# Matmuls of a constant ahead of PE's first work and in its early pauses, and the Gelu table first on ACT, in a linear-attention and feed-forward kernel

## Chip, core and metric

The kernel runs on one NeuronCore of a Trainium2 chip. The metric is device time in microseconds of one execution. Engines are named as in the profile: PE (TensorE matmul), PEld (its weight loads), DVE (VectorE), ACT (ScalarE), POOL (GpSimd), SP (SyncE, which here only issues transfers).

## The reference

A recurrent attention with a decaying state, for 4 batches, 8 heads, 768 steps and 48 dimensions per head, and a feed-forward layer with a sigmoid Gelu over the 3072 tokens of 384 features that it yields:

```python
for t in range(S):
    cur = einsum('bhd,bhe->bhde', u * k[t], v[t])
    y[t] = einsum('bhd,bhde->bhe', r[t], state + cur)
    state = w[t][..., None] * state + einsum('bhd,bhe->bhde', k[t], v[t])
x = y.transpose(0, 2, 1, 3).reshape(B * S, H * D)      # 3072 x 384
h = x @ w_in                                           # 384 x 2048
out = (h * sigmoid(1.702 * h)) @ w_out                 # 2048 x 384
```

## The kernel before

**Attention in chunks.** The 3072 steps are cut into 24 chunks of 128 steps, 6 for each batch, which follow one another through the state. Two heads share a tile, so a chunk has 4 pairs. `chunk(t)` is a Python generator of 11 pieces, the tokens `a<t>` of the order below: (1) a scan over the decays (L236) and a reciprocal; (2) a second scan (L242) and the product r*k (L249); (3) the scaled k and r (`kq`, L257 and L258), all on DVE; (4) eight matmuls of two columns (`ps_d`, L264), which read the masks `hm`; (5) the copy `s` of their result (L267) and the scaling of the state on DVE; (6) four transposes (`ps_t`, L280) and their copy `kt` on ACT (L282); (7) eight small products on ACT (`am`, L289); (8) the 64 small matmuls `ps_u` (L302, L308), then `mid` and the new state on DVE (L313, L316; for the first chunk of a batch `mid` on ACT); (9) a masked copy into `am` on DVE (L319); (10) the matmuls `ps_y` (L326 and half of L337) and a one-element copy on DVE that reads them (L346); (11) the other half of L337, and the split of the result into a high part (ACT, L202) and a low part (DVE, L203), which go to the tile `x`.

**Feed-forward.** Weights come in as pieces (`fetch`, tokens `f`), and are converted and split into high and low parts in four steps each (`convert`, tokens `w`: ACT L188 and L189, DVE L191 and L194, ACT L196, DVE L198). `first_product` (tokens `g`, 9 matmuls, L375 to L377) writes a PSUM tile `ph` out of two buffers; `gelu` (tokens `h`) reads it twice on ACT (L386, L387) and subtracts on DVE (L388); `second_product` (tokens `y`, 9 matmuls, L401 to L403) adds into `po`. The first tasks are 256 tokens wide, later ones 512. Tokens `m` are checks of magnitudes on ACT (L208), `l` are loads of a chunk, `M` is the load of the masks into `hm`, `x` moves rows of `x` to their places.

**Order.** Each engine runs its instructions in the order of the program. For the first 42 tasks that order is written by hand, in the string `RAMP` of tokens; after that a loop spreads the pieces over the tasks. A load's issue waits on the queue of its engine (SP, ACT or POOL), and later issues of that queue wait behind it.

**PSUM.** Three buffers serve all of the attention's tiles in turn (`ps_a`), two serve `ph`, three hold `po`.

**Before the order begins** POOL clears `hm`, the decays' helpers and others, DVE clears parts of two load buffers (L109, L110), and ACT runs one Gelu of a column of the mask `after` (L133), whose result nobody reads: it makes the table of functions be loaded early.

Of the kernel before, what the change touches and what calls it, by code (L numbers as in the profile page):

```python
# [8 lines left out]
F32 = mybir.dt.float32  # L9
F32R = mybir.dt.float32r  # L10
BF16 = mybir.dt.bfloat16
I32 = mybir.dt.int32
U32 = mybir.dt.uint32
AF = mybir.ActivationFunctionType
# [7 lines left out]
P = 128  # L22
# [3 lines left out]
R2 = HB + D  # L26
# [35 lines left out]

FIRST = 42
RAMP = """
l0 a0 l0 M a0 a0 l0 l1 m0 a0 f0 a0 a0 a1 a1 a0 a0 a0 m0 a1 a0 a1 a0 l1 f1 a1 a1 w0 l2 a1 m1 a1 w0 a1 a2 a1 a2
a2 w1 w0 a1 a2 a2 m1 a2 w1 m2 a2 l3 l2 a3 f2 a3 m2 w1 x1 w0 a2 a3 a3 w2 a2 f3 g0 w1 m3 l3 f4 a3 h0 g1 h1 a3 a2
y0 w3 y1 w2 w3 l4 a3 f5 a2 a3 a3 w2 m3 a3 w2 w3 a3 x3 g2 h2 w3 g3 h3 g4 y2 w4 a4 y3 f6 h4 w4 g5 w5 g6 h5 y4 w5
w4 g7 h6 w4 h7 a4 w5 y5 w5 g8 h8 w6 g9 y6 g10 y7 h9 y8 g11 f7 w6 w7 w7 h10 y9 g12 h11 w6 w6 g13 w7 l4 w7 h12
y10 h13 y11 g14 a4 f8 f9 w8 y13 g15 h14 y12 w9 l5 g16 w8 a4 h15 w9 w8 m4 w8 y14 y15 h16 g17 w9 a4 a4 g18 a5
h17 a5 f10 y16 h18 g19 g20 a5 a4 y17 w9 h19 w10 y18 w10 m4 f11 a4 l5 a5 a4 h20 l6 w11 w10 y19 l7 w11 g21 h21  # L70
m5 y20 g22 a5 w10 m5 a6 w11 a5 l6 a4 w11 a4 a5 g23 a6 a5 a5 y21 h22 a6 a6 m6 a5 a6 a7 l8 a5 a7 a6 y22 a6 a7 a6
m6 g24 a7 a6 l7 a7 h23 a7 a6 a6 a7 a7 a7 g25 l9 a7 h24 l8 a7 m7 a8 h25 y23 u a8 a8 x7 m7 y24 y25 l9 g26 m8 a8
h26 g27 h27 g28 a8 a8 y26 a8 y27 a9 a9 h28 g29 l10 y28 a8 g30 a9 m8 h29 a8 m9 g31 h30 a9 a9 l10 a9 a8 a10 a9
a8 y29 g32 y30 h31 y31 a10 a9 h32 l11 a9 g33 g34 l11 m9 a10 m10 h33 y32 g35 m10 a10 a10 a9 h34 a9 a10 l12 g36
a11 a11 y33 h35 a10 g37 a11 h36 y34 m11 h37 a10 a10 g38 a11 a11 g39 m11 a12 a10 l12 a12 a10 a12 a11 a12 a11
a12 y35 h38 y36 a11 l13 a11 a12 h39 g40 a11 m12 l13 a11 x11 y37 l14 m12 a12 y38 g41 y39 h40 a12 a13 h41 l14
"""
WIDE = 512
assert sum(CHUNKS) == NT
# [3 lines left out]
def rwkv_ffn_kernel(ctx: ExitStack, tc, wkr, vp, vrk, ub, w_in, w_out, masks, vt, uc, out):  # L83
    nc = tc.nc
    V, A, G, T = nc.vector, nc.scalar, nc.gpsimd, nc.tensor
# [4 lines left out]
    ps_h = ctx.enter_context(tc.tile_pool(name="ps_h", bufs=2, space=PSUM))  # L90
# [3 lines left out]
    at = fast.enter_context(tc.tile_pool(name="at", bufs=1))  # L94


    hm = cp.tile([R2, 2 + H], F32, name="hm")
# [6 lines left out]
    n = NP * CW + 1  # L104
# [10 lines left out]
    after = cp.tile([P, HB], F32, name="after")  # L115
# [14 lines left out]

    A.activation(at.tile([P, 1], F32, tag="s", name="junk", bufs=2), after[:, 0:1], AF.Gelu_apprx_sigmoid)  # L133

    wih, wil, woh, wol = (cp.tile([P, NF, DM], F32R, name=x) for x in ("wih", "wil", "woh", "wol"))
    acc = cp.tile([P, 2 * NT + 2 * NL], F32, name="acc")
# [39 lines left out]
    def convert(i, pool, clamp):  # L176

        s, which = divmod(i, 2)
        hi, lo = (wih, wil) if which == 0 else (woh, wol)
        n = NF * DM // NL  # L180
        hi, lo = (x.rearrange("p f m -> p (f m)")[:, s * n : (s + 1) * n] for x in (hi, lo))
        st = staged.pop(i)
        c = pool.tile([P, n], I32, tag="c", name="c", bufs=2)
        w = st.rearrange("p k (n two) -> p (k n) two", two=2)
        l, h = w[:, :, 0], w[:, :, 1]
        cf = c.bitcast(F32)
        sums = {} if clamp else dict(accum_out=acc[:, 2 * NT + i : 2 * NT + i + 1])
        A.activation(l, l.bitcast(U32), AF.Copy, scale=L_SCALE)  # L188
        A.activation(cf, h.bitcast(F32), AF.Abs, scale=W_SHIFT, **sums)  # L189
        yield  # L190
        V.scalar_tensor_tensor(h, h, -(2 ** 31), l, op0=ALU.bitwise_and, op1=ALU.bitwise_or)  # L191
        if clamp:
            V.tensor_scalar(cf, cf, W_MAX, None, op0=ALU.min)
        V.scalar_tensor_tensor(c, c, 3, h, op0=ALU.logical_shift_left, op1=ALU.bitwise_or)  # L194
        yield
        A.copy(hi, cf)  # L196
        yield
        V.tensor_tensor(lo, cf, hi.bitcast(F32), op=ALU.subtract)  # L198
        yield
# [23 lines left out]
    def chunk(t):  # L223
# [131 lines left out]
        state.pop(t - 1, None)  # L355
        yield

    def fill_x(x, c0, c1):

        for m in range(NM):  # L360
            for i, dst in enumerate((0, R2)):
                j = OFF + 2 * OFF * m + OFF * i
                (nc.sync, G)[i].dma_start(
                    x[dst : dst + OFF, :, m, c0:c1].bitcast(F32), x[j : j + OFF, :, NM, c0:c1].bitcast(F32)
                )
# [39 lines left out]
    def store(i, start, N):  # L405

        for m, o in enumerate(po.pop(i)):
            ob = pools["late"].tile([P, WIDE], F32, tag="ob", name="ob", bufs=3)[:, 0:N]
            A.activation(ob, o[:, 0:N], AF.Copy, scale=1.0 / W_SCALE)
            nc.sync.dma_start(out[m, :, bass.ds(start, N)], ob)  # L410
        xs.pop(i)
# [5 lines left out]
    with tc.manual_schedule():  # L417
        early = ExitStack()
        su = early.enter_context(tc.tile_pool(name="su", bufs=1))
        where = [(i, col) for i, n in enumerate(CHUNKS) for col in range(n)]  # L420
        starts = [sum(CHUNKS[:i]) for i in range(len(CHUNKS))]
        last = {}
        for j, task in enumerate(TASKS):
            last[task[0]] = j
        running, told = {}, {}

        def piece(kind, i):

            if (kind, i) not in running:
                running[kind, i] = {  # L430
                    "l": load, "a": chunk, "m": measures.get, "w": lambda i: convert(i, su, False)
                }[kind](i)
            next(running[kind, i])

        def do(token):
            kind, i = token[0], int(token[1:] or 0)
            told[token] = told.get(token, 0) + 1
            if kind in "lamw":
                piece(kind, i)
                if kind == "w" and all(told.get(f"w{n}") == 4 for n in range(2 * NL)):  # L440
                    early.close()
                    pools["late"] = fast.enter_context(tc.tile_pool(name="late", bufs=2))
            elif kind == "f":
                fetch(i, su)
            elif kind == "x":
                group, col = where[i]
                if i == 1:
                    fill_x(xs[group], 0, 2 * C)
                elif i == 3:
                    fill_x(xs[group], 2 * C, 4 * C)  # L450
                elif col == CHUNKS[group] - 1:
                    fill_x(xs[group], 0, (col + 1) * C)
            elif kind == "u":
                nc.sync.dma_start(u_sb, ub)
            elif kind == "M":
                nc.sync.dma_start(hm[ROWS], masks)
            elif kind == "g":
                first_product(i, TASKS[i])
            elif kind == "h":
                gelu(i, TASKS[i])  # L460
            elif kind == "y":
                second_product(i, TASKS[i])
                group = TASKS[i][0]
                if i == last[group]:
                    store(group, starts[group] * C, CHUNKS[group] * C)

        def rest():

            begins = []
            for t, (i, col) in enumerate(where):  # L470
                n = len([x for x in TASKS if x[0] == i - 1])
                begins.append(last.get(i - 1, -1) + 1 - BEFORE - round((CHUNKS[i] - 1 - col) * n / CHUNKS[i]))
            ramp = dict(told)
            for j in range(FIRST, len(TASKS) + LAG):
                for post in range(2):
                    if post and j < len(TASKS):
                        yield f"g{j}"
                        yield f"h{j}"
                    for t, begin in enumerate(begins):
                        for kind, step, half in PARTS:  # L480
                            token = f"{kind}{t + 2 * (kind == 'l')}"
                            if (step + begin, half) > (j, post) or kind == "l" and t + 2 >= NT:
                                continue
                            if ramp.get(token, 0):
                                ramp[token] -= 1
                            elif (step + begin, half) == (j, post):
                                yield token
                if j - LAG >= 0 and f"y{j - LAG}" not in told:
                    yield f"y{j - LAG}"

        for token in RAMP.split():
            do(token)
        for token in rest():
            do(token)
# [14 lines left out]
    n = nc.values_load(cnt, min_val=0, max_val=full)  # L509
# [104 lines left out]
```

## Time and profile before

| | |
|---|---|
| median of 3 runs | 546.42 us (546.21 to 547.88) |
| the profiled execution | 546.75 us |
| its span, first to last instruction | 544.8 us |
| mean granted clock of PE over the span | 0.985 |
| busy: PE, PEld | 508.0 us (93%), 421.7 us (77%) |
| busy: DVE, ACT, POOL | 283.5, 277.9, 27.0 us |
| first matmul | at 8.55 us |
| bytes moved | 45.91 MB, mean 84 GB/s |

Rows of the profile read thus. A row of the timeline has the start in us, the duration in us, the engine, the line of the source, the operation, output <- inputs, the partitions by elements, a count, and in brackets the idle time of the engine just before and what ended it. Matmuls are pipelined: a duration runs from a matmul's start to its modelled end, and the next one starts before that end, so the pace is read from the distance of starts. A row of a stretch has the window, its length, busy us and count of PE, PEld, DVE, ACT and POOL, then PE's granted clock, the share of time of the transfer engines, and GB/s. A row of waits has who waited <- for whom, the us in total, the times, and the longest.

### The profile page before, as it was taken

How to read it: one execution, taken by the hardware profiler on the slowest of the kernel's cores; microseconds unless marked ns; L12 is line 12 of the kernel's file. 1: busy time of each engine (PE TensorE's matmuls, PEld its weight loads, DVE VectorE, ACT ScalarE, POOL GpSimd, SP SyncE). 2: the span in 40 equal slices, each digit the busy share in tenths (PEclk: the TensorE clock that was granted, in tenths of full speed). 3: DMA queues.
4: the chain of work that ended last, by engine and by line, in shares of the span. 5: the costliest groups of instructions: out<-in, count | busy, mean ns of one | idle time of the engine just before them, and what ended most of it. 6: DMA issues, size and time to landing. Idle time of an engine off the chain costs nothing.

```text
span 544.8 us, 11852 instructions
## 1 busy us (share of the span) xinstructions
PE 508.0 (93%) x5014; PEld 421.7 (77%) x5014; DVE 283.5 (52%) x514; ACT 277.9 (51%) x645; POOL 27.0 (5%) x68
## 2 busy tenths in 40 slices
PE   2657899999999999999999999999999999999993
PEld 2557899988787777788888777777888887888882
DVE  6598599986555565554554554454555522111110
ACT  4578498866656346464445455445355432322231
POOL 4110110000100000000000100000100000000000
PEclk9999699999999999999999999999999999999997
DMA  8826387405423311443033143023130000200001
GB/s 209 241 66 195 105 218 226 154 2 162 131 89 88 89 46 45 116 146 88 1 89 88 37 140 87 8 82 89 42 134 1 1 1 6 82 1 1 1 0 64
DMA packets 16604, 45.91 MB, mean 84 GB/s; under 512 B 2512, under 2 KB 5904, under 8 KB 16544
## 3 DMA queue, kind: packets, MB, share of 16 engines
q1 hardware_dynamic: 13840, 34.83, 21.3%
q0 software_dynamic: 2592, 9.86, 7.3%
q8 instruction: 41, 0.67, 0.5%
q10 hardware_dynamic: 112, 0.39, 0.2%
q14 instruction: 19, 0.16, 0.1%
HBM read 38.00 MB, written 4.72 MB: 78 GB/s over the span
## 4 chain that ended last, share of the span: by engine, by line
PE 91%; DVE 4%; DMA 2%; issue 1%; POOL 0%; ACT 0%; DVEq 0%; ACTq 0%; POOLq 0%
PE po L401 13%; PE ph L375 13%; PE ph L377 12%; PE ph L376 12%; PE po L403 12%; PE po L402 12%; PE ps_y L337 5%; PE ps_y L326 3%; PE ps_u L302 2%; PE ps_u L308 2%; PE ps_t L280 2%; DMA wkr_t<-in_wkr 2%; PE ps_d L264 2%; DVE st L191 1%; DVE lp L242 1%
## 5 line engine op out<-in xcount | busy, mean ns | idle before, releaser
L388 DVE TENSOR_TENSOR gl<-gf,gh 128x512 fp32r<-128x512 f32 (+1 forms) x106 | 67.5, 639 | 191.0 <-ACT gf L387 131.6
L386 ACT ACTIVATE gh<-ph 128x512 fp32r<-128x512 f32 (+1 forms) x106 | 59.0, 557 | 190.8 <-PE ph L377 188.1
L401 PE MATMUL po<-gh,woh 128*128 128x512 f32 (+1 forms) x318 | 122.3, 384 | 0.0
L375 PE MATMUL ph<-x,wih 128*128 128x512 f32 (+1 forms) x318 | 121.0, 381 | 0.0
L377 PE MATMUL ph<-x,wil 128*128 128x512 f32 (+1 forms) x318 | 119.6, 376 | 0.0
L376 PE MATMUL ph<-x,wih 128*128 128x512 f32 (+1 forms) x318 | 119.3, 375 | 0.0
L402 PE MATMUL po<-gh,wol 128*128 128x512 f32 (+1 forms) x318 | 117.9, 371 | 0.0
L403 PE MATMUL po<-gl,woh 128*128 128x512 f32 (+1 forms) x318 | 117.9, 371 | 0.0
L377 PEld LDWEIGHTS ph<-x,wil 128*128 128x128 f32 x318 | 61.4, 193 | 11.0
L375 PEld LDWEIGHTS ph<-x,wih 128*128 128x128 f32 x318 | 61.4, 193 | 10.8
L376 PEld LDWEIGHTS ph<-x,wih 128*128 128x128 f32 x318 | 61.5, 193 | 10.3
L401 PEld LDWEIGHTS po<-gh,woh 128*128 128x128 f32 x318 | 59.9, 188 | 11.2
L403 PEld LDWEIGHTS po<-gl,woh 128*128 128x128 f32 x318 | 59.9, 188 | 10.7
L402 PEld LDWEIGHTS po<-gh,wol 128*128 128x128 f32 x318 | 60.0, 189 | 9.2
L387 ACT ACTIVATE gf<-ph 128x512 f32<-128x512 f32 (+1 forms) x106 | 58.7, 554 | 0.0
L289 ACT ACTIVATE am<-same,s 128x64 f32<-128x64 f32 x192 | 48.7, 351 | 0.1
L337 PE MATMUL ps_y<-kq,mid 48*48 48x64 f32 (+1 forms) x384 | 33.5, 232 | 3.2 <-DVE mid L346 3.2
L337 PEld LDWEIGHTS ps_y<-kq,mid 48*48 48x48 f32 (+1 forms) x384 | 27.7, 137 | 8.8 <-DVE mid L346 4.7
L202 ACT CAST x<-ps_y 112x256 fp32r<-112x256 f32 x48 | 15.7, 380 | 33.4 <-PE ps_y L337 29.1
L236 DVE TENSOR_TENSOR_SCAN lp<-wkr_t,d1r 112x516 f32<-112x516 f32 x24 | 29.4, 1225 | 3.6 <-DMA wkr_t<-in_wkr 2.9
L242 DVE TENSOR_TENSOR_SCAN lp<-wkr_t,d1f 112x516 f32<-112x516 f32 x24 | 29.4, 1224 | 0.2
L337 PE MATMUL ps_y<-kq,sf 64*64 64x64 f32 (+1 forms) x320 | 27.1, 229 | 0.0
(71 smaller groups left out, 513.4 us busy)
## 6 DMA issues: line engine op xcount, KB each, us to landing
wkr_t<-in_wkr POOLq DMA_DIRECT2D x12, 577.9 KB, 4.8
wkr_t<-in_wkr SPq DMA_DIRECT2D x11, 577.9 KB, 4.9
st<-in_w_out SPq DMA_DIRECT2D x6, 1024.0 KB, 5.0
rk_t<-in_vrk SPq DMA_DIRECT2D x16, 384.0 KB, 3.7
v_t<-in_vrk SPq DMA_DIRECT2D x24, 192.0 KB, 4.4
st<-in_w_in SPq DMA_DIRECT2D x6, 768.0 KB, 8.8
out_t<-ob SPq DMA_DIRECT2D x18, 256.0 KB, 2.7
st<-in_w_in POOLq DMA_DIRECT2D x12, 128.0 KB, 7.6
```

The source lines that it names most:

```text
L242: V.tensor_tensor_scan(pm.rearrange("r p c -> r (p c)"), w0, d1f.rearrange("r p c -> r (p c)"), 0.0, op0=ALU.mult, op1=ALU.add,)
L289: A.activation(x_[:, p], same, AF.Copy, scale=s[:, 2 * p + h : 2 * p + h + 1])
L337: T.matmul(ps[b][head(h), p], from_[head(h), p * D + OFF * h : p * D + HB], qf[head(h), p, blocks[b]], start=False, stop=p == NP - 1, skip ...
L375: T.matmul(ph, h_, xs[i][:, 0, c, cs], start=c == 0, stop=False)
L376: T.matmul(ph, h_, xs[i][:, 1, c, cs], start=False, stop=False)
L377: T.matmul(ph, l_, xs[i][:, 0, c, cs], start=False, stop=c == NM - 1)
L386: A.activation(gh, ph, AF.Gelu_apprx_sigmoid, scale=1.0 / W_SCALE)
L387: A.activation(gf, ph, AF.Gelu_apprx_sigmoid, scale=1.0 / W_SCALE)
L388: V.tensor_tensor(gl, gf, gh.bitcast(F32), op=ALU.subtract)
L401: T.matmul(o, woh[:, f, ms], gh, start=first, stop=False, skip_group_check=True)
L402: T.matmul(o, wol[:, f, ms], gh, start=False, stop=False, skip_group_check=True)
L403: T.matmul(o, woh[:, f, ms], gl, start=False, stop=f == NF - 1, skip_group_check=True)
```

## The change

Three edits:

- A tile `warm` of 128 x 512 bf16 ones is made by a memset on DVE. A new function `keep_warm(n)` takes a tile `ph` of PSUM and issues n matmuls of `warm` with itself into it, 512 columns each; nothing reads the result.
- Tokens `d<n>` in the hand-written order call it: d20 ahead of chunk 0's `ps_d`, d3 after its transposes, d12 ahead of its `ps_y`, d3 after chunk 1's transposes, d18 ahead of its `ps_y`, d3 ahead of chunk 2's `ps_d`, d4 after its transposes, d12 ahead of chunk 3's `ps_d`: 75 matmuls, all ahead of the first `first_product`. Without them the order of tokens is the same as before.
- The Gelu without a reader on ACT reads a column of `hm` instead of one of `after`. `hm` is the first tile that POOL clears. The load of the masks into `hm` comes later in the program.

```diff
-    A.activation(at.tile([P, 1], F32, tag="s", name="junk", bufs=2), after[:, 0:1], AF.Gelu_apprx_sigmoid)
+    A.activation(at.tile([R2, 1], F32, tag="s", name="junk", bufs=2), hm[:, 0:1], AF.Gelu_apprx_sigmoid)
+    warm = at.tile([P, WIDE], BF16, name="warm")
+    V.memset(warm, 1.0)
...
+    def keep_warm(n):
+
+        ph = ps_h.tile([P, WIDE], F32, tag="ph", name="ph")
+        for _ in range(n):
+            T.matmul(ph, warm[:, 0:P], warm, start=True, stop=True)
...
+            elif kind == "d":
+                keep_warm(i)
```

The start of the order, before and after (the rest differs in no token):

```diff
-l0 a0 l0 M a0 a0 l0 l1 m0 a0 f0 a0 a0 a1 a1 a0 a0 a0 m0 a1 a0 a1 a0 l1 f1 a1 a1 w0 l2 a1 m1 a1 w0 a1 a2 a1 a2
-a2 w1 w0 a1 a2 a2 m1 a2 w1 m2 a2 l3 l2 a3 f2 a3 m2 w1 x1 w0 a2 a3 a3 w2 a2 f3 g0
+l0 a0 l0 M a0 a0 d20 l0 l1 m0 a0 f0 a0 a0 d3 a1 a1 a0 a0 d12 a0 m0 a1 a0 a1 a0 l1 f1 a1 a1 d3 w0 l2 a1 m1 a1
+d18 w0 a1 a2 a1 a2 a2 w1 w0 a1 d3 a2 a2 m1 a2 d4 w1 m2 a2 l3 l2 a3 f2 a3 m2 w1 x1 w0 a2 d12 a3 a3 w2 a2 f3 g0
```

More of the change, by code (lines that the diff above doesn't have):

```diff
@@ L64 @@
 RAMP = """
-l0 a0 l0 M a0 a0 l0 l1 m0 a0 f0 a0 a0 a1 a1 a0 a0 a0 m0 a1 a0 a1 a0 l1 f1 a1 a1 w0 l2 a1 m1 a1 w0 a1 a2 a1 a2
[L66 to L74, printed above, removed]
@@ L75 @@
-a11 a11 y33 h35 a10 g37 a11 h36 y34 m11 h37 a10 a10 g38 a11 a11 g39 m11 a12 a10 l12 a12 a10 a12 a11 a12 a11
-a12 y35 h38 y36 a11 l13 a11 a12 h39 g40 a11 m12 l13 a11 x11 y37 l14 m12 a12 y38 g41 y39 h40 a12 a13 h41 l14
+l0 a0 l0 M a0 a0 d20 l0 l1 m0 a0 f0 a0 a0 d3 a1 a1 a0 a0 d12 a0 m0 a1 a0 a1 a0 l1 f1 a1 a1 d3 w0 l2 a1 m1 a1
+d18 w0 a1 a2 a1 a2 a2 w1 w0 a1 d3 a2 a2 m1 a2 d4 w1 m2 a2 l3 l2 a3 f2 a3 m2 w1 x1 w0 a2 d12 a3 a3 w2 a2 f3 g0
+w1 m3 l3 f4 a3 h0 g1 h1 a3 a2 y0 w3 y1 w2 w3 l4 a3 f5 a2 a3 a3 w2 m3 a3 w2 w3 a3 x3 g2 h2 w3 g3 h3 g4 y2 w4 a4
@@ new lines @@
+y3 f6 h4 w4 g5 w5 g6 h5 y4 w5 w4 g7 h6 w4 h7 a4 w5 y5 w5 g8 h8 w6 g9 y6 g10 y7 h9 y8 g11 f7 w6 w7 w7 h10 y9
+g12 h11 w6 w6 g13 w7 l4 w7 h12 y10 h13 y11 g14 a4 f8 f9 w8 y13 g15 h14 y12 w9 l5 g16 w8 a4 h15 w9 w8 m4 w8 y14
+y15 h16 g17 w9 a4 a4 g18 a5 h17 a5 f10 y16 h18 g19 g20 a5 a4 y17 w9 h19 w10 y18 w10 m4 f11 a4 l5 a5 a4 h20 l6
+w11 w10 y19 l7 w11 g21 h21 m5 y20 g22 a5 w10 m5 a6 w11 a5 l6 a4 w11 a4 a5 g23 a6 a5 a5 y21 h22 a6 a6 m6 a5 a6
+a7 l8 a5 a7 a6 y22 a6 a7 a6 m6 g24 a7 a6 l7 a7 h23 a7 a6 a6 a7 a7 a7 g25 l9 a7 h24 l8 a7 m7 a8 h25 y23 u a8 a8
@@ L77 @@
+x7 m7 y24 y25 l9 g26 m8 a8 h26 g27 h27 g28 a8 a8 y26 a8 y27 a9 a9 h28 g29 l10 y28 a8 g30 a9 m8 h29 a8 m9 g31
+h30 a9 a9 l10 a9 a8 a10 a9 a8 y29 g32 y30 h31 y31 a10 a9 h32 l11 a9 g33 g34 l11 m9 a10 m10 h33 y32 g35 m10 a10
+a10 a9 h34 a9 a10 l12 g36 a11 a11 y33 h35 a10 g37 a11 h36 y34 m11 h37 a10 a10 g38 a11 a11 g39 m11 a12 a10 l12
+a12 a10 a12 a11 a12 a11 a12 y35 h38 y36 a11 l13 a11 a12 h39 g40 a11 m12 l13 a11 x11 y37 l14 m12 a12 y38 g41
+y39 h40 a12 a13 h41 l14
 """
```

## The prediction

> **What bounds the kernel now.** I read the slices of the whole span first, then who waited for whom after 64 us, then single stretches, then the order of time on PE, DVE and ACT in the first 65 us.
>
> ```profile
> PEclk9999699999999999999999999999999999999997
> PE ps_y L337 <- DVE mid L346: 2.5, 8, 0.3
> 54.00:54.50 0.50, 0.04 (x4) 0.04 (x4) 0.50 (x3) 0.50 (x2) 0.00 (x0) 0.86 1.03 426
> 64.50:65.00 0.50, 0.50 (x6) 0.50 (x6) 0.50 (x2) 0.00 (x0) 0.50 (x2) 0.90 0.45 121
> 80.00:100.00 20.00, 20.00 (x169) 19.99 (x168) 19.66 (x27) 17.45 (x39) 0.99 (x2) 1.00 0.84 239
> ```
>
> From 64 us to the end PE waited 2.5 us in all (second row, the only one PE has there), so the end is PE's stream, and it moves by whatever PE gains before about 64 us. DVE is 98% busy in 80 to 100 us (last row): PE may gain only what DVE gains too. The recorded clock falls to half at 54.36 (0.86 over the half microsecond) and is full again from 64.6. Before its first fall the record says full, but the matmuls do not:
>
> ```profile
> 43.26 0.56 PE L375 MATMUL ph<-x,wih 128*128 128x256 f32 x1
> 44.05 0.41 PE L375 MATMUL ph<-x,wih 128*128 128x256 f32 x1
> 44.26 0.41 PE L376 MATMUL ph<-x,wih 128*128 128x256 f32 x1
> 47.25 0.69 PE L280 MATMUL ps_t<-ident,kq 112*128 112x112 f32 x4
> 61.46 0.58 PE L375 MATMUL ph<-x,wih 128*128 128x256 f32 x1
> 65.09 0.28 PE L375 MATMUL ph<-x,wih 128*128 128x256 f32 x1
> 65.21 0.28 PE L376 MATMUL ph<-x,wih 128*128 128x256 f32 x1
> ```
>
> Starts of 256 columns are 0.21 us apart at 44 us and 0.12 at 65 us: at 44 us PE ran at half speed. So it is slow from its first matmul to about 47.4 us (the transposes at 47.25 are already mostly fast), some 4.1 us after the dense stream began at 43.26, and again from 54.36 to 64.6, 3.1 us after dense products set in at 61.46. The same work at half and at full speed:
>
> ```profile
> 18.80 1.86 PE L264 MATMUL ps_d<-hm,rku 112*128 112x2 f32 x8
> 92.25 0.95 PE L264 MATMUL ps_d<-hm,rku 112*128 112x2 f32 x8
> 21.65 1.01 PE L280 MATMUL ps_t<-ident,kq 112*128 112x112 f32 x4
> 96.38 0.55 PE L280 MATMUL ps_t<-ident,kq 112*128 112x112 f32 x4
> 23.33 0.99 PE L302 MATMUL ps_u<-v_t,kt 64*64 64x48 f32 x30 [0.68 <-ACT kt L282]
> 24.18 1.12 PE L308 MATMUL ps_u<-kq 64*64 64x64 f32 x30
> 104.31 0.62 PE L302 MATMUL ps_u<-v_t,kt 64*64 64x48 f32 x30
> 104.82 0.65 PE L308 MATMUL ps_u<-kq 64*64 64x64 f32 x30
> 29.41 1.13 PE L326 MATMUL ps_y<-am,v_t 64*48 64x64 f32 x32 [4.10 <-DVE am L319]
> 31.07 0.31 PE L337 MATMUL ps_y<-kq,sf 64*64 64x64 f32 x1
> 114.09 0.69 PE L326 MATMUL ps_y<-am,v_t 64*48 64x64 f32 x32
> 115.02 0.22 PE L337 MATMUL ps_y<-kq,sf 64*64 64x64 f32 x1
> ```
>
> ps_d 1.86 to 0.95, ps_t 1.01 to 0.55, ps_u 1.97 (23.33 to 25.30) to 1.16, ps_y's first part 1.97 (29.41 to 31.38) to 1.15. The small matmuls do not raise the clock themselves: PE works from 16.92 to 22.66 without a pause and ps_u at 23.33 is still slow.
>
> Where the early stage waits, on PE (first fence) and on DVE (second),
>
> ```profile
> 8.55 1.84 PE L264 MATMUL ps_d<-hm,rku 112*128 112x2 f32 x8 [8.55 <-DVE rku L249]
> 16.92 1.13 PE L326 MATMUL ps_y<-am,v_t 64*48 64x64 f32 x32 [2.56 <-DVE am L319]
> 41.57 1.83 PE L264 MATMUL ps_d<-hm,rku 112*128 112x2 f32 x8 [2.77 <-DVE rku L249]
> 54.46 0.98 PE L302 MATMUL ps_u<-v_t,kt 64*64 64x48 f32 x27 [2.39 <-DVE x L203]
> ```
>
> ```profile
> 3.26 0.91 DVE L110 MEMSET wkr_t<- 16x1024 f32 x1 [0.16 <-issue]
> 5.14 1.24 DVE L236 TENSOR_TENSOR_SCAN lp<-wkr_t,d1r 112x516 f32<-112x516 f32 x1 [0.97 <-DMA wkr_t<-in_wkr]
> 12.53 1.23 DVE L236 TENSOR_TENSOR_SCAN lp<-wkr_t,d1r 112x516 f32<-112x516 f32 x1 [1.94 <-DMA wkr_t<-in_wkr]
> 25.37 0.36 DVE L313 TENSOR_TENSOR mid<-ps_u,sf 112x192 f32<-112x192 f32 x1 [2.45 <-PE ps_u L308]
> 31.44 0.21 DVE L346 COPY_PREDICATED_SCALAR mid<-after,ps_y 1x1 f32 x1 [0.84 <-PE ps_y L337]
> 43.35 0.36 DVE L316 TENSOR_TENSOR sf<-ps_u,mid 112x192 f32<-112x192 f32 x1 [0.53 <-DVE mid L313]
> 46.63 0.15 DVE L267 COPY s<-ps_d 128x8 f32<-128x8 f32 x1
> 48.18 0.43 DVE L388 TENSOR_TENSOR gl<-gf,gh 128x256 fp32r<-128x256 f32 x1 [0.80 <-ACT gf L387]
> ```
>
> and on ACT and SP:
>
> ```profile
> 7.95 1.28 ACT L208 ACT_TABLE_LOAD   x1 [7.95 <-DVE lp L242]
> 10.41 1.28 ACT L133 ACT_TABLE_LOAD   x1
> 22.74 0.53 ACT L282 COPY kt<-ps_t 128x448 f32<-128x448 f32 x1 [0.62 <-PE ps_t L280]
> 1.29 0.41 SPq L456 DMA_DIRECT2D hm<-in_masks  x1
> ```
>
> Between 25 and 54 us DVE is busy but for the waits shown: DVE leads there, and only what PE keeps it waiting for can be won.
>
> **The change part by part.** *The price of a dummy.* No row shows a bf16 matmul of 512 columns. Two of 256 columns cost 0.425 us at half and 0.24 at full speed; I take these, and as bounds half and double. *d20.* The memset of warm follows the last one of DVE (ends 4.17), costs at most about 0.49 us (half of L110's 0.91 for 1024 elements, estimated) and fits into the 0.97 before the scan at 5.14: nothing on the path. So d20 starts near 4.65. With 4.1 us at half speed (9.6 of them) and the other 10.4 at 0.24 it takes 6.6 and ends near 11.3, where the real ps_d was ready at 8.55. ps_d then ends at 12.25 instead of 10.39, and DVE's copy of s, which stands ahead of the scan of chunk 1, at about 12.5. That scan waits for its load until 12.53 and had 1.94 of idle time before it: the delay is hidden, just. Without that cover it is paid one for one; all at half speed d20 ends at 13.2, ps_d at 15.0, and the scan is 2.7 late.
>
> *To 17 us.* ps_t, its copy, ps_u and d12 follow: 12.1 + 0.5 + 0.6 + 1.2 + 12 x 0.24 = 17.3; ps_y was let go at 16.92 by DVE, so 0.3 is lost. d3 costs nothing, as PE waits for ACT's kt beside it. *17 to 25 us.* 16.92 to 22.66 is 5.74 of slow PE work without a pause; by the pairs above (ratios 0.51 to 0.58) it takes 3.2, a gain of 2.5, and ps_u gives 0.8 more. Less 0.3, DVE's L313 starts 3.0 earlier, near 22.4. ACT's kt (22.74), and the weight conversions behind it, move by some 2.3, which still feeds DVE's L191 in time to within 0.1. *25 to 49 us.* d18 takes 4.3, about the pause of 4.10 that DVE sets, so it costs at most 0.2, which lies beside DVE's scan. Then the waits of DVE go: 0.84 at 31.44 (0.75 of it, for that 0.2), 0.53 at 43.35, and 0.80 at 48.18, as the first products take 9 x 0.12 = 1.1 instead of 9 x 0.21 = 1.9 each. What is late next is ps_y of chunk 2: its PSUM buffer is freed by the s copy at 46.63 in DVE's order, so the wait that DVE has for it right after 48.6 stays as it is. Sum at 49.2, where DVE starts the third conversion: 3.0 + 0.75 + 0.53 + 0.80 = 5.1. The second d12 and d4 lie in pauses that DVE sets (2.77 at 41.57), with ps_u finished sooner than before.
>
> *49 to 65 us.* Nothing is put into the pause before 54.46. PE reaches it sooner while DVE holds it as before, so the pause grows from 2.39 to over 3; I take the clock to fall again and the rest to run as before: 0. Bounds: it stays full, and ps_u 0.8, ps_y 0.8 + 0.4 and the slow first products to 64.6 (3.1 us, 1.4 saved) give 3.4; or the next dense stretch raises it only after 4.1 us, as the first one did, and half of that one more microsecond, 0.5, is lost.
>
> The Trainium skill, TensorE: Matmul & The Clock Gate, Part 1, says that the clock rises after a busy window and falls after an idle one, in free-running windows of 3.413 us. The fall at 54.36 and the rise at 64.6 lie 10.24 us apart, three such windows, so the trace agrees. By it d20 would take 3.4 to 6.8 us at half speed and end between 10.9 and 12.4; the upper end would make the early scan 1 late.
>
> *ACT and SP.* One of two table loads of 1.28 goes, the other moves before ACT's first work at 7.95. Alone it makes kt of chunk 0 earlier, which the load awaited at 12.53 hides: 0. The masks' load (L456, SP) must now wait for the Gelu instruction, which reads hm: from 1.29 to about 2.7 behind ACT's load issue, the table and the read. The loads of v and weights queued behind it on SP slip by 1.4. ps_d, which needs the masks, now starts at 11.3; the first conversion on ACT is near 20.5. Cost 0 to 1.4, taken 0. PSUM buffers of ph are not yet in use when the last dummy is done, and no one reads them: 0.
>
> Sum: -5.1 against the profiled execution, whose time is 546.75 (span 544.8 and 1.95 around it): 541.65. The median of the three runs, 546.42, is 0.33 below it: 541.3.
>
> **The rivals.** *Slower: the dummies do not raise the clock.* At 0.425 each d20 makes chunk 1 2.7 late, d12 takes 5.1 in a pause of 2.56, d18 7.65 in 4.10, the second d12 5.1 in 2.77: 2.7 + 2.5 + 3.5 + 2.3 = 11, so 557.8. It turns at 0.21 to 0.23 us each (2.56 / 12, 4.10 / 18): above that a block outlasts its pause. For it: small matmuls never raised the clock. Against: dense ones did at 47.4 and 64.6.
>
> *The clock falls between the blocks.* If it falls after the first d12, the 3.0 goes, and d18, which must raise it anew (4.1 + 8.4 x 0.24 = 6.1), outlasts its pause by 2.0; the later 2.1 makes up for it: 546.7, no change. If it falls only after d18, 543 to 545. For it: the fall at 54.36 came although PE had small work until 52. Against: no bare pause over 2 us stays, and from 47.4 to 52 small work mixed with dense kept the clock full.
>
> By the same page and section, half speed returns after a window of idle time, about 3.4 us; no run so far shows what share of work is enough to keep it.
>
> *The clock also survives the pause at 52 to 54 us*: 3.4 more, 537.9. Against: the pause grows.
>
> *The gain is not carried past 65 us*, because DVE, 98% busy, or a load cannot follow: no change, 546. Against: DVE's and ACT's streams move by the same 5.
>
> **How the numbers follow.** Forecast 0.55; also past the pause 0.15; a fall between blocks 0.17 (half of it no change); no rise 0.06; not carried 0.07. What differs by under 0.3% (1.6 us) cannot be told from no change here. Faster: 0.55 + 0.15 + 0.10 = 0.80; same 0.07 + 0.05 = 0.12; slower 0.08. The range takes the forecast, the pause and the late falls: the 537.9 less 0.5 for what the dummies may outlast their pauses by (0.3 and 0.2 above), so 537.4, to 544.5. The forecast alone has 540.8 to 542.8: that 0.5 not lost, or 1.0 for a late d20 and 0.5 for a late rise.
>
> **What would show it.** First products near 39 us at 0.12 apart; ps_y of chunk 0 still near 17; DVE's L313 near 22.4, L191 of the third conversion near 44 instead of 49.2; PE's ps_u of chunk 3 about 5 earlier and at half speed soon after. Wrong: ps_u or ps_y at 1.97 inside 12 to 45 us, or dummy blocks followed by late real matmuls.

## The result, and the profile after

The changed kernel takes 540.74 us (median of 4 runs, 540.61 to 541.59) against 546.32 us before on the same chip (546.01 to 547.88): ratio 0.9895, 95% interval 0.9874 to 0.9917. On a second chip it was 540.58 against 546.91, ratio 0.9877 (0.9856 to 0.9897). The forecast was 541.3, with a range of 537.4 to 544.5. The profiled execution took 541.59, its span 539.6; all places below are from it. Line numbers: L133 is now L134; after it they are 3 higher than before up to the attention's end (L264 is L267, L313 is L316, L337 is L340, L346 is L349) and 9 higher in the feed-forward part (L375 is L384); the dummies, as the matmuls without a reader are called here, are L365.

Here are the slices' clock from the page, the one row that PE has in the waits after 60 us, and the stretches in which the clock changes (columns as before, the clock third from the end):

```profile
PEclk9997799999999999999999999999999999999998
PE ps_y L340 <- DVE mid L349: 2.5, 8, 0.3
38.00:40.00 2.00, 2.00 (x17) 2.00 (x18) 1.89 (x5) 1.79 (x4) 0.00 (x0) 0.95 0.93 331
42.00:44.00 2.00, 2.00 (x51) 1.89 (x51) 1.31 (x7) 1.95 (x3) 0.00 (x0) 0.69 1.01 242
50.00:51.00 1.00, 0.53 (x23) 0.34 (x13) 0.36 (x1) 0.38 (x1) 0.00 (x0) 0.53 0.72 291
60.00:61.00 1.00, 1.00 (x9) 1.00 (x9) 0.64 (x3) 1.00 (x3) 0.00 (x0) 0.85 0.90 188
```

PE's late stream is as tight as it was, with the same 2.5 us of waits: the end moved because its beginning moved. The clock falls at 39.8, rises at 43.2, falls at 50.06 and rises at 60.3 (each worked out from the mean of its stretch: 0.95 over 2 us is 1.8 us full and 0.2 half). Before its first recorded fall the paces of the matmuls must tell again. PE's order of time:

```profile
4.76 6.61 PE L365 MATMUL ph<-warm 128*128 128x512 bf16 x20 [4.76 <-DVE warm L136]
11.21 0.95 PE L267 MATMUL ps_d<-hm,rku 112*128 112x2 f32 x8
17.01 0.69 PE L329 MATMUL ps_y<-am,v_t 64*48 64x64 f32 x32
20.91 0.62 PE L305 MATMUL ps_u<-v_t,kt 64*64 64x48 f32 x30
21.42 0.65 PE L311 MATMUL ps_u<-kq 64*64 64x64 f32 x30
37.41 1.02 PE L267 MATMUL ps_d<-hm,rku 112*128 112x2 f32 x8 [1.12 <-DVE rku L252]
38.62 0.28 PE L386 MATMUL ph<-x,wil 128*128 128x256 f32 x1
38.74 0.28 PE L384 MATMUL ph<-x,wih 128*128 128x256 f32 x1
41.95 1.34 PE L329 MATMUL ps_y<-am,v_t 64*48 64x64 f32 x30
49.23 0.60 PE L305 MATMUL ps_u<-v_t,kt 64*64 64x48 f32 x27 [2.37 <-DVE x L206]
52.23 1.13 PE L329 MATMUL ps_y<-am,v_t 64*48 64x64 f32 x32 [1.70 <-DVE am L322]
```

ps_d takes 0.95 at 11.21 instead of 1.84, ps_u 1.16 at 20.91 (to 22.07) instead of 1.97, and the first products start 0.12 apart near 38.7: PE runs at full speed from the end of d20 to the fall at 39.8. ps_y is slow at 41.95 (1.34 for L329, 0.69 at full speed) and again at 52.23 (1.13, as at half speed). DVE, then ACT and SP:

```profile
4.22 0.48 DVE L136 MEMSET warm<- 128x512 bf16 x1
12.20 0.17 DVE L270 COPY s<-ps_d 128x8 f32<-128x8 f32 x1 [2.43 <-PE ps_d L267]
12.31 1.23 DVE L239 TENSOR_TENSOR_SCAN lp<-wkr_t,d1r 112x516 f32<-112x516 f32 x1
22.13 0.36 DVE L316 TENSOR_TENSOR mid<-ps_u,sf 112x192 f32<-112x192 f32 x1 [1.22 <-PE ps_u L311]
27.52 0.21 DVE L349 COPY_PREDICATED_SCALAR mid<-after,ps_y 1x1 f32 x1
38.78 0.36 DVE L319 TENSOR_TENSOR sf<-ps_u,mid 112x192 f32<-112x192 f32 x1
42.39 0.76 DVE L397 TENSOR_TENSOR gl<-gf,gh 128x256 fp32r<-128x256 f32 x2
43.84 0.21 DVE L349 COPY_PREDICATED_SCALAR mid<-after,ps_y 1x1 f32 x1 [0.69 <-PE ps_y L340]
43.98 1.20 DVE L194 SCALAR_TENSOR_TENSOR st<-st 128x1024 int32<-128x1024 int32 x1
60.84 1.23 DVE L239 TENSOR_TENSOR_SCAN lp<-wkr_t,d1r 112x516 f32<-112x516 f32 x1
```

```profile
1.27 1.28 ACT L134 ACT_TABLE_LOAD   x1 [1.27 <-PEq L613]
2.80 0.32 SPq L467 DMA_DIRECT2D hm<-in_masks  x1
```

In the kernel before, ACT had loaded two tables and reached the Gelu without a reader only at 11.71, behind its first check of magnitudes; so that Gelu did not load its table early there, and here it does. The waits of 0.84, 0.53 and 0.80 that the prediction wanted gone are gone (27.52, 38.78 and 42.39 stand without a bracket). The third conversion starts at 43.98; before, it and the scan of chunk 4 stood here:

```profile
49.21 1.21 DVE L191 SCALAR_TENSOR_TENSOR st<-st 128x1024 int32<-128x1024 int32 x1
66.33 1.22 DVE L236 TENSOR_TENSOR_SCAN lp<-wkr_t,d1r 112x516 f32<-112x516 f32 x1
```

So DVE is ahead by 3.2 us at L316 (25.37 to 22.13), 5.2 at the third conversion, 5.5 at chunk 4, and the span is shorter by 5.2: what is won before 49 us goes through to the end.

### The profile page after: what moved, and what is told of

Same layout as the page of the kernel before. It is cut to its first block, busy times and chain, and to the rows that moved or that the text cites. A ratio compares the mean times of both kernels' runs of the same rounds, so it can differ in the third digit from the quotient of the medians.

```text
span 539.6 us, 11994 instructions
## 1 busy us (share of the span) xinstructions
PE 516.1 (96%) x5084; PEld 420.0 (78%) x5089; DVE 283.9 (53%) x515; ACT 276.9 (51%) x644; POOL 27.0 (5%) x68
## 4 chain that ended last, share of the span: by engine, by line
PE 92%; DVE 4%; issue 1%; ACT 1%; DVEq 0%; ACTq 0%
PE po L410 13%; PE ph L384 13%; PE ph L386 13%; PE ph L385 12%; PE po L411 12%; PE po L412 12%; PE ps_y L340 5%; PE ps_y L329 3%; PE ps_u L305 2%; PE ps_u L311 2%; PE ps_t L283 2%; PE ph L365 2%; PE ps_d L267 1%; DVE st L194 1%; DVE lp L245 0%
## 5 line engine op out<-in xcount | busy, mean ns | idle before, releaser
L384 PE MATMUL ph<-x,wih 128*128 128x512 f32 (+1 forms) x318 | 120.7, 380 | 0.0
L384 PEld LDWEIGHTS ph<-x,wih 128*128 128x128 f32 x318 | 61.1, 192 | 10.7
L340 PE MATMUL ps_y<-kq,mid 48*48 48x64 f32 (+1 forms) x384 | 31.7, 224 | 3.2 <-DVE mid L349 3.2
L340 PEld LDWEIGHTS ps_y<-kq,mid 48*48 48x48 f32 (+1 forms) x384 | 26.1, 131 | 8.7 <-DVE mid L349 4.6
L205 ACT CAST x<-ps_y 112x256 fp32r<-112x256 f32 x48 | 15.8, 382 | 29.4 <-PE ps_y L340 25.5
L211 ACT ACTIVATE junk<-lp 112x1032 bf16<-112x1032 f32 x24 | 25.6, 1066 | 5.8 <-DVE lp L245 5.8
```

What stands on the lines that cost most here:

```text
L340: T.matmul(ps[b][head(h), p], from_[head(h), p * D + OFF * h : p * D + HB], qf[head(h), p, blocks[b]], start=False, stop=p == NP - 1, skip ...
L384: T.matmul(ph, h_, xs[i][:, 0, c, cs], start=c == 0, stop=False)
```

## The experiments

Each was timed beside the kernel before, in three groups. The kernel before had a median of 547.20 us with the first four kernels, 546.91 with the next four, 546.78 with the last three.

**The Gelu edit alone.** The kernel before with the one new line:

```diff
-    A.activation(at.tile([P, 1], ...), after[:, 0:1], AF.Gelu_apprx_sigmoid)
+    A.activation(at.tile([R2, 1], ...), hm[:, 0:1], AF.Gelu_apprx_sigmoid)
```

> The Gelu edit alone, no dummies. The load of chunk 1 landed at 12.41 us before and at 8.24 after, because the masks' load (1.29 to 2.80) and all that SP issues behind it came later and left the transfer engines to it. Theory A (the edit is worth something by itself): without dummies DVE's scan of chunk 1 starts right behind the s copy, near 10.6 instead of 12.53; everything up to the first slow products moves by 1.9, so 544.4. Theory B (the prediction's): the edit alone is worth 0, 546.3. The clock stays at half speed to about 45 us by both.

Measured 545.49, ratio 0.9969 (0.9958 to 0.9979): 1.7 us less by the medians (1.9 by Theory A), 1.1 by the profiled spans. The scan of chunk 1 (order of time of DVE) starts at 11.02 instead of 12.53 (near 10.6 by Theory A):

```profile
11.02 1.23 DVE L236 TENSOR_TENSOR_SCAN lp<-wkr_t,d1r 112x516 f32<-112x516 f32 x1
```

The edit is worth something by itself; Theory B, the prediction's, falls.

**The table first, the masks not held up.** Same kernel, but the Gelu reads a column of d1r:

```diff
-    ... after[:, 0:1], AF.Gelu_apprx_sigmoid)
+    ... d1r[:, 0, 0:1], AF.Gelu_apprx_sigmoid)
```

> The kernel before with the Gelu on ACT reading d1r instead of the mask column: the table loads first of all, as in the Gelu edit, but the masks' load does not wait for it and SP issues as before. Theory A (the Gelu edit alone brings 1 to 1.7 us because SP's loads come later and chunk 1's load lands near 8.3): here it lands near 12.4 and the time is that of before. Theory B (the table's place on ACT brings it): 0.997 of before, 1 to 1.7 us less.

Measured 547.06, ratio 1.0012 (0.9998 to 1.0026): nothing. The table loads at 1.28 us and the Gelu runs at 2.57 here too, as in the changed kernel, so their place on ACT brings no time. What differs is SP. Here is the time to landing of the load of chunk 1, issued at 2.44 us, in the kernel before, the Gelu edit alone, this kernel and the changed kernel, in that order:

```profile
DMA to landing us min/median/max: 10.0/10.0/10.0
```

```profile
DMA to landing us min/median/max: 5.9/5.9/5.9
```

```profile
DMA to landing us min/median/max: 9.6/9.6/9.6
```

```profile
DMA to landing us min/median/max: 5.8/5.8/5.8
```

Where the masks' load waits for the Gelu, and the loads of v and weights wait behind it on SP (1.29 to 2.80), the load of chunk 1 from POOL's queue lands 4 us sooner. The gain of this edit is an order of transfers, brought about by what the Gelu happens to read.

**The dummies alone.** The changed kernel with the old Gelu line.

> The dummies alone; the Gelu reads the old column, so the masks are loaded at 1.29 and the load of chunk 1 lands near 12.4 again. By both theories the scan of chunk 1 starts near 12.5 instead of 12.31, since d20 holds the s copy to 12.2 either way: 540.9, 0.2 over the changed kernel. If the Gelu edit brought part of the 5.2 us, this one is over 542.

Measured 541.52, ratio 0.9893 (0.9872 to 0.9914). That lies between the 540.9 expected and the 542 named for the case that the Gelu edit brought part. The dummies carry nearly all. The spans say the same, 540.2 against 539.6; the rest is the scan of chunk 1, which waits for its load here (landed at 2.44 + 10.5 = 12.94) and starts at 13.03 instead of 12.31. This kernel differs from the one before by more than the dummies: though its Gelu line is the old one, ACT loads the table at 1.28 and runs the Gelu at 5.02, ahead of its checks; no run shows why. The experiment before this one shows that this place by itself brings nothing.

**Two columns instead of 512.**

```diff
-        for _ in range(n):
-            T.matmul(ph, warm[:, 0:P], warm, start=True, stop=True)
+        for _ in range(2 * n):
+            T.matmul(ph[:, 0:2], warm[:, 0:P], warm[:, 0:2], start=True, stop=True)
```

> The changed kernel with every dummy of 512 columns replaced by two of 2 columns: PE still has work at the same places, but the array hardly any. A two-column matmul of the attention takes 0.21 us at half speed, so the blocks take at most as long as at half speed before. Theory A (the gain is the clock, and the clock follows the array's use): half speed up to about 45 us as before; the time is that of the Gelu edit alone, 545.5, or up to 4 us more where blocks outlast their pauses. Theory B (it is enough that PE has something to do): the gain stays, 541.

Measured 545.64, ratio 0.9974 (0.9959 to 0.9989): the time of the Gelu edit alone. Order of time of PE:

```profile
4.77 1.22 PE L365 MATMUL ph<-warm 128*128 128x2 bf16 x40 [4.77 <-DVE warm L136]
9.02 1.84 PE L267 MATMUL ps_d<-hm,rku 112*128 112x2 f32 x8 [3.03 <-DMA hm<-in_masks]
28.39 1.13 PE L329 MATMUL ps_y<-am,v_t 64*48 64x64 f32 x32 [3.05 <-DVE am L322]
```

These rows are at half speed, ps_d at 1.84. Twice as many matmuls at the same places, and no gain beyond that of the Gelu edit. But the blocks are also short here (1.22 us for 40), so this does not part little use of the array from little time.

**d20 alone**, the other seven blocks left out.

> The changed kernel with d20 alone; the other seven blocks are left out. Theory A (small matmuls and bare pauses do not hold the clock): it falls again at one of the first windows after 15 us; little of PE's work is at full speed, and the time is 544.5 to 545.5. Theory B (once up, small work and pauses of up to 4 us hold it): the gain stays, 541.

Measured 546.70, ratio 0.9992 (0.9978 to 1.0006). Stretches of this kernel, and a row of PE's order of time:

```profile
12.00:16.00 4.00, 1.72 (x70) 1.37 (x69) 3.77 (x7) 3.40 (x11) 0.00 (x0) 0.98 1.03 345
16.00:20.00 4.00, 3.35 (x47) 3.23 (x48) 2.23 (x6) 0.67 (x3) 1.53 (x3) 0.50 1.04 275
```

```profile
16.65 1.13 PE L328 MATMUL ps_y<-am,v_t 64*48 64x64 f32 x32 [2.31 <-DVE am L321]
```

The clock falls at 15.8, some 1.5 us into the pause of 2.31 us that d12 fills in the changed kernel, and 3.35 us of small work in the next 4 do not bring it back. Theory B falls. The time is 1.2 over what Theory A allowed: d20 holds the scan of chunk 1 until 12.27 here, where it starts at 11.02 with the Gelu edit alone, and little of that is won back: the `mid` of chunk 1 starts at 25.10 against 24.35, and the spans are 544.5 against 543.7. Added to d20, the seven blocks in the pauses bring the 6.1 us between this kernel and the changed one; whether they would do so without d20 no run shows.

**The memset of warm first on DVE**, so that d20 starts earlier:

```diff
+    warm = at.tile([P, WIDE], BF16, name="warm")
+    V.memset(warm, 1.0)
     for x in wkr_t:
         V.memset(x[0:OFF, 0:n], 1.0)
```

> The changed kernel with the memset of warm ahead of DVE's other memsets: d20 runs from about 1.6 to 8.2 us instead of 4.76 to 11.2 and holds nobody. Theory A (in the changed kernel d20 is on the path: DVE idles 2.43 us before the s copy, and the load of chunk 1 has been there since 8.24): the scan of chunk 1 starts near 9.9 instead of 12.31, and 2.4 us go through to the end: 538.3. Theory B (the delay is hidden, as the prediction had it, by the load or by the later weight loads): 540.7.

Measured 539.17 (538.25 to 539.66), ratio 0.9851 (0.9832 to 0.9870).

```profile
1.54 7.41 PE L365 MATMUL ph<-warm 128*128 128x512 bf16 x20 [1.54 <-DVE warm L110]
9.92 1.23 DVE L239 TENSOR_TENSOR_SCAN lp<-wkr_t,d1r 112x516 f32<-112x516 f32 x1
```

The scan of chunk 1 starts 2.4 earlier, as Theory A has it; of that the medians show 1.4 to 1.6 (Theory A: all of it), the profiled spans 3.3 (536.3), where the fall at 39.8 happens to be missing.

**Two more blocks, in the pauses at 47 and 51 us:**

```diff
-... a3 f5 a2 a3 a3 w2 m3 a3 w2 w3 a3 x3 ...
+... a3 f5 a2 d10 a3 a3 w2 m3 d7 a3 w2 w3 a3 x3 ...
```

> The changed kernel with two more blocks, d10 ahead of chunk 3's ps_u and d7 ahead of its ps_y, in the pauses of 2.37 and 1.70 us that were left bare. Theory A (the clock falls at 50.06 because of these pauses): it stays full; chunk 3's ps_y takes 1.15 instead of 1.97, its second half 0.7 instead of 1.1, and the products from 55.5 to 60.3 run at 0.12 instead of 0.21, 2.1 saved: 3.3 in all, 537.4. Theory B (it falls for another reason, or DVE takes over): 540.7 or, where the blocks outlast the pauses, a little more.

Measured 538.32 (538.17 to 540.13), ratio 0.9850 (0.9828 to 0.9872), 2.3 to 2.4 under the medians of the changed kernel (3.3 by Theory A); the slowest of these five runs is still under the fastest of the changed kernel, 540.42. Stretches:

```profile
48.00:52.00 4.00, 3.92 (x80) 2.11 (x82) 2.74 (x7) 2.21 (x4) 0.00 (x0) 1.00 0.64 248
52.00:56.00 4.00, 3.68 (x81) 3.48 (x81) 2.09 (x4) 1.30 (x4) 0.45 (x1) 1.00 0.02 4
```

Full clock where the changed kernel has half: with these pauses filled, that fall does not come.

**Both together.**

> The early memset and the two late blocks together. Theory A (they act at different places, one on DVE's wait at 12 us, the other on the clock after 50): their gains add, 2.4 + 3.2 under the changed kernel, 535.1. Theory B (DVE, busy nearly without a pause from 60 us on, takes over): nearer 537.5.

Measured 535.98 (535.06 to 537.25), ratio 0.9799 (0.9779 to 0.9820): the gains add (the measured 1.5 + 2.4 make 536.8 of the 540.7). It lies between the theories' 535.1 and 537.5, nearer to A. This beats the changed kernel by 4.6 us.

**The last bare pause filled too:** the second d12 made d17.

> The early memset and the two late blocks, and the second d12 made d17, which fills the 1.12 us that PE still waits ahead of chunk 3's ps_d. Theory A (that bare pause and the ps_d of little use behind it make the fall near 39.8 that the changed kernel shows, in some executions): the median is that of the best execution without it, 535.1, and the spread (535.06 to 537.25 without it) is smaller. Theory B (those runs differ for another reason): 536.0 as before; and where d17 outlasts the pause, 0.1 to 0.3 more.

Measured 535.60 (535.14 to 536.28), ratio 0.9797 (0.9779 to 0.9816), not to be told from the one before; the spread is smaller, 1.1 against 2.2 us, which five runs each do not settle. Its profiled execution, the slowest of its five, shows a fall elsewhere:

```profile
28.00:32.00 4.00, 3.58 (x75) 2.71 (x76) 3.96 (x8) 2.99 (x10) 1.51 (x4) 0.78 0.23 53
32.00:36.00 4.00, 3.67 (x15) 1.61 (x16) 3.93 (x6) 3.88 (x8) 1.00 (x2) 0.80 0.85 289
26.80:30.20 3.40, 2.59 (x24) 1.81 (x26) 3.40 (x8) 2.39 (x6) 0.94 (x2) 1.00 0.01 4
```

The clock falls at 30.2 and is back at 33.6. In the 3.4 us up to the fall (last row) PE counts as busy for 2.59. Filling this pause does not end the falls; what it does to their number is inconclusive.

**Zeros instead of ones in warm.**

> The changed kernel with zeros in warm instead of ones. Theory A (the clock follows that the array is occupied, not what passes through it): d20 turns fast after 3 to 7 us and the time is 540.6 as with ones. Theory B (it follows the data's activity): half speed all through, blocks at 0.425 each outlast their pauses, 550 or more.

Measured 540.46, ratio 0.9887 (0.9870 to 0.9904): as with ones. Whether ones or zeros pass through the array makes no difference.

## Why the prediction was right, point by point

**The bound.** Right: PE's stream after 64 us moved as a whole, and its waits stayed at 2.5 us.

**The price of a dummy, d20.** Taken at 0.425 and 0.24 us. Where a block was recorded whole (with the dummies alone), 18 took 4.06 and 12 took 2.76 us, so one costs 1.30 / 6 = 0.217 at full speed; d20's 6.61 us make ten at half and ten at full speed (10 x 0.425 + 10 x 0.217 = 6.4, and the last one's drain). Predicted 6.6 and an end near 11.3; measured 11.37. The memset cost 0.48 and was hidden; half of the 0.91 it was estimated from is 0.46, not the 0.49 written.

**The cover of d20's delay.** This step failed, and so did the one on the Gelu edit; the two errors cancelled. The delay was to hide behind the load of chunk 1 until 12.53. That load was there at 8.24, because SP's slip, priced at 0 to 1.4 of loss, was a gain. So the cover was gone, and DVE stood idle for 2.43 us before the s copy at 12.20; yet the scan started at 12.31, next to the forecast 12.5. The early memset shows the 2.4 us that lay there, and the Gelu edit alone is worth 1.7 us where no dummy uses them up. That the two errors met within 0.2 us is luck.

**17 to 49 us.** L316 3.2 earlier (3.0 forecast), the third conversion 5.2 (5.1). The wait for ps_y that was to stay as it was is 0.69 at 43.84 instead of 0.47: the clock fell at 39.8 for 3.4 us. That is the rival of a fall between the blocks, in its late form, and ps_y at 41.95, whose first part took 1.85 us (to 43.80) instead of 1.15, is nearly the sign of being wrong that the prediction named. It was cheap, not the 543 to 545 of that rival, since DVE led there. With the early memset the clock did not fall there, and the same wait was 0.25.

**49 to 65 us.** Taken as 0 and nearly so. One reading failed: the pause was to grow from 2.39 to over 3, and it is 2.37, since DVE came as much earlier as PE; the clock fell all the same. For the rest: ps_u ran at full speed until 50.06, 0.7 gained (L316 for chunk 3 at 50.58, 5.9 earlier), and the rise at 60.3 came 4.7 us behind the start of the dense products at 55.56 (3.1 before), 0.4 lost again (chunk 4's scan is 5.5 earlier). That it is the bare pauses that let the clock fall there is shown by the two late blocks.

**The rivals.** That the dummies do not raise the clock is refuted, that the gain is lost to DVE as well; the clock past the pause came only with more blocks, and then brought 2.4 of the 3.4 us named. The 557.8 of the first is 11 on the profiled 546.75; on the median, as the forecast is given, it is 557.4.

On the clock's windows the Trainium skill (TensorE: Matmul & The Clock Gate, Part 1) agrees: the changed kernel's changes at 39.8, 43.2, 50.06 and 60.3 lie 3.4, 6.8 and 10.2 us apart, one, two and three times its 3.413. The advice of the Trainium skill in the same part, no idle gap above about 3.4 us, is too mild here: with small work around them, the first 1.5 us of a pause (before ps_y with d20 alone) and a pause of 2.37 us (at 46.9 to 49.2) were enough.

## What to carry to other kernels

Read the granted clock from the paces of like matmuls, since the record said full speed while PE ran at half until 47 us. Where PE waits in an early phase for another engine, matmuls without a reader can keep its clock up, if each block is no longer than its pause and the first one starts early enough to be done before real work; filling only the start was worth nothing here. And an edit that makes one small load wait can pay or cost through the loads queued behind it: ask which other transfer gets the room.

## What the runs showed of the hardware that was not expected

SP's loads behind the masks, issued 1.4 to 1.9 us later, let one load of POOL's queue land after 5.8 to 5.9 us instead of 9.6 to 10.0 (10.5 with the dummies alone).

The time that PE counts as busy does not tell whether the clock stays. Two stretches of the changed kernel, each 3.4 us long and ending where a change can come, if the steps of 3.4 us are carried back from the fall at 39.8:

```profile
26.15:29.57 3.42, 2.42 (x66) 1.76 (x68) 3.38 (x7) 3.42 (x7) 0.00 (x0) 1.00 0.02 6
36.40:39.81 3.41, 2.40 (x21) 2.43 (x21) 3.30 (x7) 3.20 (x5) 0.00 (x0) 1.00 1.00 311
```

PE is equally busy in both; behind the first the clock stayed full, behind the second it fell. The second holds 1.02 us of ps_d, matmuls of two columns, and so does the stretch before the fall at 30.2 with d17; the first holds none. That such matmuls count for little fits the blocks of two columns above, but is argued, not shown. What share of use is enough the runs do not settle.
